# Two expert layers on one core: groups of 256 inner units as the outer loop over all tokens, with the sums in SBUF

## The chip, the cores and the metric

One core of a Trainium2 chip runs the whole program. The metric is the time of one execution on the device in microseconds (us). Engines are named as in the profile: PE is TensorE's products, PEld its loads of the stationary operand, DVE VectorE, ACT ScalarE, POOL GpSimd, SP the engine whose queue issues the DMAs.

## What is computed

Attention over 4 batches, 8 heads, 576 tokens and a head width of 64 (weights below a threshold near the row's greatest are dropped) gives x, 2304 tokens of 512 values. Two expert layers follow, each with 2048 inner units:

```
h = x @ w_in              # 2304 x 512 times 512 x 2048
g = h * sigmoid(1.702 h)  # layer 1;   layer 2: g = max(0.01 h, h)
x = g @ w_out             # 2304 x 2048 times 2048 x 512
```

The weights arrive as float64. The output is float32.

## The kernel before, in words

Products run on TensorE in fp32r, and so that little precision is lost each operand is kept as a high half and a low half: x = xh + xl, w = wh + wl, g = gh + gl. A product is the sum of three: high by high, high by low, low by high. This is why each pass over a 128 x 128 piece of weights costs three matmuls.

The attention (to about 398 us) is ordered by hand in the table START. It is untouched by the change, but for how x is declared (one tile with four parts in place of four tiles). It also converts the weights of the first three blocks of 128 inner units (f = 0, 1, 2) of layer 1, as NA = 3 says.

In the expert layers the order of each engine's instructions is laid out when the program is built, by a planner that goes by the program's order and by when it expects operands and buffers to be ready; on the chip each engine then keeps to that order.

**Weights.** `load_weights` (line 327 on) fetches a block f: `stage` (L286) issues two DMAs of 512 KB on SP's queue into one of three staging buffers (w64), and `convert` turns each of the two pieces from float64 words into float32: ACT takes the magnitude (L300), then DVE runs four operations (L302, L304, L308, L312) on a float buffer wF (two of them), then ACT rounds to the high half (L322) and POOL subtracts to get the low half (L325). The halves (wih, wil, woh, wol) of f = 3 to 15 have 13 slots in the pool wb, so all of a layer's weights are resident.

**Layer 1** runs over five blocks of tokens (WIDTHS: 496, 436, 440, 436, 496), and inside each over the 16 blocks f. For each pair (block, f):
- `split_x` (L816), once for each block: four copies on ACT (L830, xh) and four subtractions on DVE (L828, xl).
- `hidden` (L833): 12 matmuls (L840) into a PSUM buffer h (four of them), ACT's sigmoid (L847), DVE's product gf of h and it (L848), ACT's rounding gh (L852), POOL's subtraction gl (L854).
- `product` (L857): 12 matmuls (L872) into four PSUM accumulators y which stay open over all 16 f.

After the last f, `finish` (L876) copies the four y into x (L881), half on ACT, half on DVE.

**Layer 2** is the same over six blocks of 384 tokens (TILES), with 9 output matmuls of 512 columns for each f (L874; here g is the stationary operand and rows of the output come out), DVE's gf at L851 after ACT's L850, and `finish` copies (L885) and stores (L887, L890).

The loop at L892 to L911 issues hidden one f ahead of product. It loads the weights of f = 5 to 15 of layer 1 during layer 1's first block of tokens, two f ahead (L901), and the weights of all 16 f of layer 2 during layer 1's last block, each f after its last use (L909).

Of the kernel before, what the change touches and what calls it, by code (L numbers as in the profile page):

```python
# [23 lines left out]
NA = 3  # blocks of 128 hidden units whose first weights have room during the attention  # L24
SB = 3  # staging buffers
TB = 496  # tokens of a block at the most
# Blocks of tokens: the first layer's by their widths, the second's as three tiles of rows of the
# output, (batch, i) for rows 4p + i and (batch, 4) for the last 64 rows of two batches.
WIDTHS = (496, 436, 440, 436, 496)
TILES = [[(b, i) for i in range(3)] for b in range(3)]  # L30
TILES += [[(0, 3), (1, 3), (2, 3)], [(3, 3), (0, 4), (2, 4)], [(3, 0), (3, 1), (3, 2)]]
HI_MAX = 15 * 2.0**13 - 2.0**-7  # of a float64's high word as float32, where the value is float32's greatest
# How a tile of probabilities gets its low part: "D" VectorE; "P" GpSimd, from a copy; "PP" GpSimd
# makes both parts from the copy.
LO = ("P", "P", "PP", "P", "D", "P", "D", "P", "P")
# the engine of each threshold, the buffers of v, of the probabilities and of the scores, and the
# products that bring TensorE to speed
# [4 lines left out]
# The order of the attention phase's steps, by position: a pair of heads starts PERIOD after the one  # L42
# before it, and pairs with an order of their own have it under their number.
# [196 lines left out]
def attention_moe_moe(  # L240
# [23 lines left out]
    x = [cp.tile([P, NTOK], F32, name=f"x{c}") for c in range(NCB)]  # L264

    # tau as a threshold offset that is never negative, and the scale of the scores:
    # with tau < 0 nothing reaches the threshold and every key weighs the same.
# [9 lines left out]
    def stage(layer, f, n):  # L277
        """A block of weights of 128 hidden units on its way into SBUF."""
        m = 2 if wide else 1
        w = weights[layer][n].bitcast(I32) if wide else weights[layer][n]  # L280
        if n == 0:
            src = w[:, f * P * m : (f + 1) * P * m].rearrange("(c p) x -> p c x", p=P)
        else:
            src = w[f * P : (f + 1) * P, :].rearrange("p (c x) -> p c x", c=NCB)
        t = stg.tile([P, DM * m], I32 if wide else F32, tag="w64", name=f"w{layer}_{f}_{n}", bufs=SB)
        nc.sync.dma_start(split(t, NCB), src)  # L286
        staged[layer, f, n] = t

    def convert(layer, f, n, part):
        src = staged[layer, f, n]  # L290
        if wide:
            # float64 to float32 by bits, magnitudes brought into float32's range
# [42 lines left out]
    # A pair of heads shares its tiles of 128 tokens: 0-3 the first head's, 4 the last 64 tokens  # L335
    # of both, 5-8 the second head's. Column i * 128 + p of x is token 4p + i of a batch, and
    # column 512 + r is token 512 + r.
    with tc.tile_pool(name="at", bufs=1) as at, tc.manual_schedule():
# [74 lines left out]
        # tiles of scores: head and block of 128 rows; the middle one has the last 64 rows of both  # L413
# [101 lines left out]
        def halves(p, t):  # L515
            """Source bank and the two destinations of a tile's transposed probabilities."""
# [36 lines left out]
        def corner(pt, src):  # L553
            """Both 64 by 64 halves of src transposed, each in its own partitions."""
# [151 lines left out]
        # The first pair's operands are made by whichever engine is free: the second head's tiles  # L706
        # (part A) before the rest (part B), and both orders of the halves of k instead of a swap.
# [69 lines left out]
        # the activation table and TensorE's clock are up before the first operands come  # L777
# [17 lines left out]
    ml = ctx.enter_context(tc.tile_pool(name="ml", bufs=2, reuse_waits="tile"))  # L795
    wb = ctx.enter_context(tc.tile_pool(name="wb", bufs=NF - NA, reuse_waits="tile"))

    xs_of, g_of, y_of = {}, {}, {}

    def pieces(layer, blk):  # L800
        """Columns of a block and, for each run of them, where they are in x."""
        if layer == 1:
            c0 = sum(WIDTHS[:blk])
            w = WIDTHS[blk]
            return w, [(slice(0, w), 1, lambda t: t[:, c0 : c0 + w])]
        (b, i), second = TILES[blk][:2]
        if second == (b, i + 1):
            return 384, [(slice(0, 384), 1, lambda t: t[:, b * S : b * S + 384])]
        if i == second[1]:
            return 384, [(slice(0, 384), 3, lambda t: split(t, B)[:, b : b + 3, i * P : i * P + P])]  # L810
        return 384, [
            (slice(0, P), 1, lambda t: t[:, b * S + i * P : b * S + i * P + P]),
            (slice(P, 384), 4, lambda t: split(t, B)[:, :, 512:S]),
        ]

    def split_x(layer, blk):  # L816
        w, runs = pieces(layer, blk)
        hs, ls = (
            [ml.tile([P, TB], F32R, tag=f"x{n}{c}", name=f"x{n}{layer}_{blk}_{c}", bufs=1)[:, 0:w] for c in range(NCB)]
            for n in "hl"  # L820
        )
        for low in range(2):
            for c in range(NCB):
                for cols, n, at_x in runs:
                    src = at_x(x[c])
                    hi, lo = (t[c][:, cols] if n == 1 else split(t[c][:, cols], n) for t in (hs, ls))
                    if low:
                        nc.vector.tensor_tensor(out=lo, in0=src, in1=hi, op=ALU.subtract)  # L828
                    else:
                        nc.scalar.copy(hi, src)  # L830
        xs_of[layer, blk] = (w, hs, ls)

    def hidden(layer, blk, f):  # L833
# [10 lines left out]
        gh = ml.tile([P, TB], F32R, tag="gh", name=f"gh{n}")[:, 0:w]  # L844
        gl = ml.tile([P, TB], F32R, tag="gl", name=f"gl{n}")[:, 0:w]
# [7 lines left out]
        last = (layer, blk, f) == units[-1]  # L853
# [3 lines left out]
    def product(layer, blk, f):  # L857
        w = xs_of[layer, blk][0]
        gh, gl = g_of.pop((layer, blk, f))
        woh, wol = wslot[layer, f][2:4]  # L860
        if f == 0:
            two = [ps.tile([P, 2, 512], F32, tag="s", name=f"y{layer}_{blk}_{e}", bufs=2) for e in range(2)]
            y_of[layer, blk] = [two[e // 2][:, e % 2, :] for e in range(NCB if layer == 1 else w // P)]
        ys = y_of[layer, blk]
        terms = [(i, e) for i in range(3) for e in range(len(ys))]
        if (layer, blk, f) == units[-1]:
            terms.sort(key=lambda z: z[1])
        for i, e in terms:
            wt, g = ((woh, gh), (wol, gh), (woh, gl))[i]
            first, last = f == 0 and i == 0, f == NF - 1 and i == 2  # L870
            if layer == 1:
                nc.tensor.matmul(ys[e][:, 0:w], lhsT=wt[:, e * P : (e + 1) * P], rhs=g, start=first, stop=last)  # L872
            else:
                nc.tensor.matmul(ys[e], lhsT=g[:, e * P : (e + 1) * P], rhs=wt, start=first, stop=last)  # L874

    def finish(layer, blk):  # L876
        ys = y_of.pop((layer, blk))
        if layer == 1:
            w, ((_, _, at_x),) = pieces(layer, blk)
            for e, y in enumerate(ys):  # L880
                (nc.vector.tensor_copy if e % 2 else nc.scalar.copy)(at_x(x[e]), y[:, 0:w])  # L881
            return
        for e, (y, (b, i)) in enumerate(zip(ys, TILES[blk])):
            o = stg.tile([P, 2 * DM], F32, tag="w64", name=f"o{blk}_{e}", bufs=SB)[:, 0:DM]
            (nc.vector.tensor_copy if e % 2 else nc.scalar.copy)(o, y)  # L885
            if i < 4:
                nc.sync.dma_start(out[b * S : b * S + 512, :].rearrange("(p i) e -> p i e", i=4)[:, i, :], o)  # L887
            else:
                for j in range(2):
                    nc.sync.dma_start(out[(b + j) * S + 512 : (b + j + 1) * S, :], o[64 * j : 64 * j + 64, :])  # L890

    units = [(l, blk, f) for l, n in ((1, len(WIDTHS)), (2, len(TILES))) for blk in range(n) for f in range(NF)]  # L892
    split_x(1, 0)
    for f in range(NA, NF):
        if f < NA + 2:
            load_weights(1, f)
    hidden(*units[0])
    for n, u in enumerate(units):
        l, blk, f = u
        if l == 1 and blk == 0 and f + 2 >= NA + 2 and f + 2 < NF:  # L900
            load_weights(1, f + 2)  # L901
        if n + 1 < len(units):
            nl, nb, nf = units[n + 1]
            if nf == 0:
                split_x(nl, nb)
            hidden(nl, nb, nf)
# [33 lines left out]
```

## Time and profile before

| what | us |
|---|---|
| median of three runs (1257.3 to 1259.44) | 1257.49 |
| span of the profiled execution, first to last instruction | 1252.7 |
| what lies between the two | 4.8 |
| first matmul of the expert layers | 397.68 |
| TensorE busy in the span | 1190.8 |

The page gives no time of the profiled execution beside its span. To read the profile: a busy share is the time that an engine has at least one instruction in work. Matmuls overlap one another (a new one enters while the one before drains), so the length of one matmul is longer than the distance to the next, and the distance is what counts. The granted clock of TensorE is given as a share of its full speed of 2.4 GHz.

### The profile page before, as it was taken

The numbers are of one execution on the slowest core, as the hardware profiler recorded it, in microseconds if no ns is written. First come the engines' busy times: TensorE is split into PE (matmuls) and PEld (weight loads), VectorE is DVE, ScalarE is ACT, GpSimd is POOL, SyncE is SP. The second block draws the span as 40 slices with busy tenths as digits, with TensorE's granted clock in tenths as the row PEclk, the third lists the DMA queues.
The fourth block names the chain that finished last, engine by engine and source line by source line (L and its number), as shares of the span: only waits on it lengthen the run. The fifth ranks groups of instructions, "written<-read, shape, count | busy, mean of one in ns | idle before, by whom it ended". The sixth has DMA issues, their size and how long they took to land.

```text
span 1252.7 us, 17393 instructions
## 1 busy us (share of the span) xinstructions
PE 1190.8 (95%) x6361; PEld 1033.3 (82%) x6361; DVE 703.1 (56%) x1322; ACT 603.3 (48%) x1133; POOL 640.8 (51%) x583
## 2 busy tenths in 40 slices
PE   6989999999998888999999999888999999999998
PEld 5778888888776665999999988667999999999987
DVE  7899999999999988512112138898121212121211
ACT  6778888888885544323222244445222323232322
POOL 5899999999986555322222235555222222222221
PEclk9799999999999999999999999999999999999999
DMA  4422213232112343200000003432000000000100
GB/s 129 117 63 70 74 50 87 56 76 68 48 30 67 119 125 128 66 1 1 1 1 1 1 18 118 133 110 77 1 26 1 26 1 26 1 26 1 26 1 26
DMA packets 47493, 62.40 MB, mean 50 GB/s; under 512 B 10416, under 2 KB 39088, under 8 KB 47408
## 3 DMA queue, kind: packets, MB, share of 16 engines
q1 hardware_dynamic: 47408, 61.29, 16.8%
q8 instruction: 50, 0.82, 0.3%
q14 instruction: 35, 0.29, 0.1%
HBM read 47.71 MB, written 4.72 MB: 42 GB/s over the span
## 4 chain that ended last, share of the span: by engine, by line
PE 56%; POOL 18%; DVE 17%; issue 5%; ACT 2%; DMA 1%; SPq 0%; POOLq 0%; ACTq 0%; DVEq 0%
PE h L840 25%; PE y L874 15%; PE y L872 10%; POOL ptg0l L550 5%; DVE wF L308 4%; POOL ptg1l L550 4%; DVE wF L312 3%; DVE wF L304 3%; DVE wF L302 2%; POOL thr L477 2%; PE pv L585 2%; POOL rb L634 1%; DVE pp L491 1%; POOL khl L376 1%; POOL vhl L376 1%
## 5 line engine op out<-in xcount | busy, mean ns | idle before, releaser
L854 POOL TENSOR_TENSOR gl<-gf,gh 128x384 fp32r<-128x384 f32 (+3 forms) x175 | 199.4, 1140 | 475.9 <-ACT gh L852 403.8
L851 DVE TENSOR_TENSOR gf<-h,gf 128x384 f32<-128x384 f32 x96 | 53.4, 556 | 287.5 <-ACT gf L850 287.5
L840 PE MATMUL h<-xh,wih 128*128 128x384 f32 (+3 forms) x704 | 168.0, 355 | 13.6 <-ACT wih L322 7.6
L840 PE MATMUL h<-xh,wil 128*128 128x384 f32 (+3 forms) x704 | 176.3, 355 | 1.2 <-POOL wil L325 1.2
L840 PE MATMUL h<-xl,wih 128*128 128x384 f32 (+3 forms) x704 | 169.3, 354 | 0.1
L852 ACT CAST gh<-gf 128x384 fp32r<-128x384 f32 (+3 forms) x176 | 95.1, 541 | 118.5 <-DVE gf L851 46.2
L491 DVE SCALAR_TENSOR_TENSOR pp<-sc,thr,e 128x576 f32<-128x576 f32 x128 | 150.7, 1186 | 1.7 <-POOL thr L477 1.1
L840 PEld LDWEIGHTS h<-xh,wih 128*128 128x128 f32 x704 | 128.5, 188 | 26.5 <-ACT wih L322 10.9
L848 DVE TENSOR_TENSOR gf<-h,gf 128x496 f32<-128x496 f32 (+2 forms) x80 | 50.5, 633 | 172.9 <-ACT gf L847 172.8
L850 ACT ACTIVATE gf<-h 128x384 f32<-128x384 f32 x96 | 47.3, 492 | 199.7 <-PE h L840 199.1
L840 PEld LDWEIGHTS h<-xl,wih 128*128 128x128 f32 x704 | 130.1, 189 | 12.7 <-DVE xl L828 0.5
L840 PEld LDWEIGHTS h<-xh,wil 128*128 128x128 f32 x704 | 129.2, 189 | 12.6 <-POOL wil L325 3.7
L470 ACT ACTIVATE e<-s,m 128x576 f32<-128x576 f32 x144 | 107.2, 745 | 33.6 <-DVE sc L457 18.9
L457 DVE TENSOR_SCALAR_CACHE_REDUCE sc<-s 128x576 f32<-128x576 f32 x144 | 107.1, 750 | 6.9 <-PE s L429 3.8
L429 PE MATMUL s<-kt,qt 128*128 128x288 f32 x512 | 99.1, 320 | 10.4 <-ACT e L470 8.0
L847 ACT ACTIVATE gf<-h 128x496 f32<-128x496 f32 (+2 forms) x80 | 44.1, 553 | 119.5 <-PE h L840 117.7
L872 PE MATMUL y<-gh,woh 128*128 128x496 f32 (+2 forms) x320 | 83.0, 379 | 12.5 <-ACT gh L852 12.4
L550 POOL TENSOR_TENSOR ptg0l<-raw,ptg0h 128x512 fp32r<-128x512 f32 x64 | 92.1, 1441 | 0.3 <-ACT ptg0h L543 0.3
L429 PEld LDWEIGHTS s<-kt,qt 128*128 128x128 f32 x512 | 73.3, 191 | 17.2 <-ACT e L470 14.4
L874 PE MATMUL y<-woh,gh 128*128 128x512 f32 x288 | 82.8, 394 | 3.9 <-DVE x L881 2.6
L512 PE MATMUL pp<-ident,pp 128*128 128x128 f32 x512 | 79.1, 283 | 5.9 <-DVE pp L491 4.4
L874 PE MATMUL y<-woh,gl 128*128 128x512 f32 x288 | 83.2, 396 | 0.9 <-POOL gl L854 0.9
(122 smaller groups left out, 2250.4 us busy)
## 6 DMA issues: line engine op xcount, KB each, us to landing
w<-in_moe_w_in_dram SPq DMA_DIRECT2D x32, 512.0 KB, 3.7
w<-in_moe_w_out_dram SPq DMA_DIRECT2D x32, 512.0 KB, 3.5
kt<-kt SPq DMA_DIRECT2D x30, 288.0 KB, 4.1
kn<-in_k_dram SPq DMA_DIRECT2D x16, 256.0 KB, 2.9
qn<-in_q_dram SPq DMA_DIRECT2D x16, 256.0 KB, 2.8
vn<-in_v_dram SPq DMA_DIRECT2D x16, 256.0 KB, 3.0
out_dram<-o SPq DMA_DIRECT2D x16, 256.0 KB, 2.3
kn<-in_k_dram SPq DMA_DIRECT2D x32, 16.0 KB, 2.6
```

Source lines behind the costliest of these rows:

```text
L429: nc.tensor.matmul(sc[:, a, 0:HALF], lhsT=w, rhs=kt[n][:, c : c + HALF], start=n == 0, stop=n == 1)
L457: nc.vector.tensor_scalar(out=split(r["sc", t], 2), in0=r["s", t][:, :, 0:HALF], scalar1=1.0, scalar2=3.0e38, op0=ALU.mult, op1=ALU.min, a ...
L470: nc.scalar.activation(split(e, 2), r.pop(("s", t))[:, :, 0:HALF], AF.Exp, bias=r["m"][:, t : t + 1], scale=-1.0)
L491: nc.vector.scalar_tensor_tensor(out=dst, in0=r.pop(("sc", t)), scalar=r["thr"][:, t : t + 1], in1=r.pop(("e", t)), op0=ALU.is_le, op1=ALU ...
L512: nc.tensor.transpose(pt[:, j * P : (j + 1) * P], src[:, off + j * P : off + (j + 1) * P], ident)
L550: nc.gpsimd.tensor_tensor(out=lo, in0=split(st[p].pop(("raw", t)), 4), in1=hi, op=ALU.subtract)
L840: nc.tensor.matmul(h, lhsT=wt[:, c * P : (c + 1) * P], rhs=xx[c], start=i == 0 and c == 0, stop=i == 2 and c == NCB - 1)
L851: nc.vector.tensor_tensor(out=gf, in0=h, in1=gf, op=ALU.max)
L852: nc.scalar.copy(gh, gf)
L854: (nc.vector if last else nc.gpsimd).tensor_tensor(out=gl, in0=gf, in1=gh, op=ALU.subtract)
L872: nc.tensor.matmul(ys[e][:, 0:w], lhsT=wt[:, e * P : (e + 1) * P], rhs=g, start=first, stop=last)
L874: nc.tensor.matmul(ys[e], lhsT=g[:, e * P : (e + 1) * P], rhs=wt, start=first, stop=last)
```

## The change

In the expert layers the loops change places. The outer loop is now over groups of G = 2 blocks f, 256 inner units, eight groups for each layer; the inner loop is over all tokens, in five blocks of at most 512 (four of 512, one of 256), in both layers. What is resident changes with it: the xh and xl of all tokens are kept (a buffer for each block of tokens), and wb has four slots in place of 13. PSUM now sums over one group only (six matmuls for each output tile), and the tile is then added to a sum in SBUF, which lies in x itself: group 0 copies (half on ACT, half on DVE), later groups add on DVE. In the last group of layer 2 the DVE add writes the output tile o, which is stored in pieces of consecutive rows. y has two buffers, one for each output tile in work, gh and gl four each. Weights are loaded two groups ahead of their use, in the first two steps of each group. Comments are removed too. The core of the diff:

```diff
-NA = 3  # blocks of 128 hidden units whose first weights have room during the attention
-TB = 496  # tokens of a block at the most
-WIDTHS = (496, 436, 440, 436, 496)
+TB = 512
+G = 2
...
-    x = [cp.tile([P, NTOK], F32, name=f"x{c}") for c in range(NCB)]
+    xx_all = cp.tile([P, NCB, NTOK], F32, name="x")
+    x = [xx_all[:, c, :] for c in range(NCB)]
...
-    wb = ctx.enter_context(tc.tile_pool(name="wb", bufs=NF - NA, reuse_waits="tile"))
+    wb = ctx.enter_context(tc.tile_pool(name="wb", bufs=2 * G, reuse_waits="tile"))
...
+    def product(layer, grp, blk, e):
         w = xs_of[layer, blk][0]
+        cols = span(blk)
+        y = ps.tile([P, 2, 512], F32, tag="s", name=f"y{layer}_{grp}_{blk}_{e}", bufs=2)[:, 0, :]
+        n = 0
+        for i in range(3):
+            for f in range(grp * G, grp * G + G):
+                gh, gl = g_of[layer, blk, f]
+                woh, wol = wslot[layer, f][2:4]
+                wt, g = ((woh, gh), (wol, gh), (woh, gl))[i]
...
+                if layer == 1:
+                    nc.tensor.matmul(y[:, 0:w], lhsT=wt[:, at_e], rhs=g, start=first, stop=last)
+                else:
+                    nc.tensor.matmul(y, lhsT=g[:, at_e], rhs=wt, start=first, stop=last)
...
+        if grp == 0:
+            (nc.vector.tensor_copy if e % 2 else nc.scalar.copy)(acc, y)
+        elif layer == 1 or grp < NF // G - 1:
+            nc.vector.tensor_tensor(out=acc, in0=y, in1=acc, op=ALU.add)
+        else:
             o = stg.tile([P, 2 * DM], F32, tag="w64", name=f"o{blk}_{e}", bufs=SB)[:, 0:DM]
+            nc.vector.tensor_tensor(out=o if w == TB else split(o, 2), in0=y, in1=acc, op=ALU.add)
+            store(o, cols.start + e * P)
...
+    steps = [(l, g, blk) for l in (1, 2) for g in range(NF // G) for blk in range(NB)]
...
+    weights_until(2 * G)
+    lead(steps[0])
+    lead(steps[1])
+    for j in range(G):
+        hidden(*steps[0], j)
+    for n, (l, g, blk) in enumerate(steps):
+        nxt = steps[n + 1] if n + 1 < len(steps) else None
+        if n + 2 < len(steps):
+            lead(steps[n + 2])
+        ne = outputs(l, blk)
+        per = (ne + G - 1) // G
+        for j in range(G):
+            if nxt:
+                hidden(*nxt, j)
+            for e in range(j * per, min(ne, (j + 1) * per)):
+                product(l, g, blk, e)
+        if blk < G:
+            weights_until((((l - 1) * NF) // G + g + 1) * G + G + blk + 1)
```

`lead` calls `split_x` for a block of tokens in group 0 of a layer, `weights_until(n)` calls `load_weights` up to the n-th block of both layers, and `outputs` gives the output tiles of a block of tokens: four, or two for the narrow block of layer 2.

## Rows read from the trace of the kernel before

**Rows 1.** The profile page: the span, the busy time of each engine with its share of the span, and TensorE's busy tenths in 40 slices of 31.3 us.
```profile
span 1252.7 us, 17393 instructions
...
PE 1190.8 (95%) x6361; PEld 1033.3 (82%) x6361; DVE 703.1 (56%) x1322; ACT 603.3 (48%) x1133; POOL 640.8 (51%) x583
...
PE   6989999999998888999999999888999999999998
```
**Rows 2.** Busy times by stretch of the expert layers. Columns: the stretch, its length, then for PE, PEld, DVE, ACT and POOL the busy us and the number of instructions, TensorE's granted clock, the DMA engines' busy share, GB/s.
```profile
397.70:510.00 112.30, 95.50 (x392) 72.54 (x393) 102.19 (x130) 53.72 (x91) 58.31 (x41) 0.98 0.39 122
510.00:738.00 228.00, 228.00 (x1145) 214.72 (x1144) 42.83 (x72) 61.84 (x115) 55.47 (x49) 1.00 0.02 5
738.00:850.00 112.00, 101.71 (x439) 83.02 (x437) 94.86 (x122) 54.68 (x95) 60.26 (x43) 0.97 0.37 113
850.00:920.00 70.00, 66.02 (x325) 58.41 (x326) 30.47 (x47) 25.15 (x51) 25.46 (x22) 1.00 0.10 31
920.00:1247.50 327.50, 327.50 (x1640) 296.15 (x1638) 54.32 (x103) 88.56 (x185) 79.37 (x78) 1.00 0.03 11
```
**Rows 3.** What TensorE waited for, from 396 to 560 us (first four) and from 700 to 900 us (the last); from 900 us to the end this view has no row. Columns: us in total, times, the longest.
```profile
PE h L840 <- ACT wih L322: 7.6, 7, 2.0
PE y L872 <- ACT gh L852: 5.2, 6, 1.4
PE h L840 <- DVE gf L848: 2.1, 1, 2.1
PE h L840 <- ACT xh L830: 1.6, 1, 1.6
...
PE y L874 <- DVE x L881: 2.6, 1, 2.6
```
**Rows 4.** ACT's timeline: the copies of finished sums that end a block of tokens, five of layer 1 and the first two of layer 2. Columns: start, busy us, what.
```profile
515.45 1.04 ACT L881 COPY x<-y 128x496 f32<-128x496 f32 x2
...
589.53 0.95 ACT L881 COPY x<-y 128x436 f32<-128x436 f32 x2 [1.14 <-PE y L872]
...
665.99 0.96 ACT L881 COPY x<-y 128x440 f32<-128x440 f32 x2 [1.15 <-PE y L872]
...
742.91 0.94 ACT L881 COPY x<-y 128x436 f32<-128x436 f32 x2
...
848.68 1.04 ACT L881 COPY x<-y 128x496 f32<-128x496 f32 x2
...
916.90 1.08 ACT L885 COPY o<-y 128x512 f32<-128x512 f32 x2 [0.70 <-PE y L874]
...
983.86 1.07 ACT L885 COPY o<-y 128x512 f32<-128x512 f32 x2 [0.70 <-PE y L874]
```
**Rows 5.** The timeline at the start of the expert layers (their first matmuls, and ACT's table load ahead of the first sigmoid) and at their end (the last two matmuls).
```profile
397.68 1.17 PE L840 MATMUL h<-xh,wih 128*128 128x496 f32 x4 [1.62 <-ACT xh L830]
...
408.14 1.28 ACT L847 ACT_TABLE_LOAD   x1
...
1247.03 0.63 PE L874 MATMUL y<-woh,gl 128*128 128x512 f32 x2
```
**Rows 6.** The source line L585, the attention's products of 256 columns: the durations in ns of a weight load, of a matmul and of a separate semaphore step on TensorE (least, median, greatest).
```profile
L585 PEld LDWEIGHTS pv<-ptg0h,vhl x128: 186/188/333, 32.9 to 387.7; 128*128 128x128 f32 x128
L585 PE MATMUL pv<-ptg0h,vhl x128: 274/283/581, 33.1 to 387.8; 128*128 128x256 f32 x128
...
L585 PEldq EVENT_SEMAPHORE  x34: 51/51/51, 32.1 to 391.2; - x34
```
**Rows 7.** TensorE's timeline in the attention (the first row) and in layer 2 (the others): runs of four matmuls, with the start of the first and the time from there to the end of the fourth.
```profile
204.65 0.64 PE L585 MATMUL pv<-ptg0h,vhl 128*128 128x256 f32 x4
...
1002.73 0.86 PE L840 MATMUL h<-xh,wih 128*128 128x384 f32 x4
1003.43 0.86 PE L840 MATMUL h<-xh,wil 128*128 128x384 f32 x4
```
**Rows 8.** VectorE's groups of instructions from 397.7 us to the end. Columns: busy us and mean ns of one, then the idle time before them.
```profile
L308 DVE SCALAR_TENSOR_TENSOR wF<-w,wF 128x512 int32<-128x512 int32 x58 | 64.5, 1113 | 1.3
...
L312 DVE SCALAR_TENSOR_TENSOR wF<-w,wF 128x512 int32<-128x512 int32 x58 | 51.8, 892 | 1.2
L848 DVE TENSOR_TENSOR gf<-h,gf 128x496 f32<-128x496 f32 (+2 forms) x80 | 50.5, 633 | 172.9 <-ACT gf L847 172.8
L304 DVE TENSOR_SCALAR wF<-wF 128x512 int32<-128x512 int32 x57 | 47.3, 830 | 1.2
L302 DVE TENSOR_SCALAR wF<-wF 128x512 f32<-128x512 f32 x57 | 34.5, 605 | 21.6 <-ACT wF L300 21.6
...
L885 DVE COPY o<-y 128x512 f32<-128x512 f32 x6 | 4.1, 692 | 11.9 <-ACT o L885 11.9
```
**Rows 9.** VectorE's timeline in the first layer's last block: one conversion of a piece of weights (L302, L304, L308, L312) and a product gf (L848).
```profile
787.31 0.42 DVE L302 TENSOR_SCALAR wF<-wF 128x512 f32<-128x512 f32 x1
787.77 0.43 DVE L304 TENSOR_SCALAR wF<-wF 128x512 int32<-128x512 int32 x1
788.23 1.74 DVE L308 SCALAR_TENSOR_TENSOR wF<-w,wF 128x512 int32<-128x512 int32 x1
789.89 0.66 DVE L848 TENSOR_TENSOR gf<-h,gf 128x496 f32<-128x496 f32 x1
790.47 0.68 DVE L312 SCALAR_TENSOR_TENSOR wF<-w,wF 128x512 int32<-128x512 int32 x1
```

More of the change, by code (lines that the diff above doesn't have):

```diff
@@ L25 @@
 SB = 3
-TB = 496
-WIDTHS = (496, 436, 440, 436, 496)
-TILES = [[(b, i) for i in range(3)] for b in range(3)]
-TILES += [[(0, 3), (1, 3), (2, 3)], [(3, 3), (0, 4), (2, 4)], [(3, 0), (3, 1), (3, 2)]]
+TB = 512
+G = 2
 HI_MAX = 15 * 2.0**13 - 2.0**-7
@@ L795, in attention_moe_moe, with span @@
     ml = ctx.enter_context(tc.tile_pool(name="ml", bufs=2, reuse_waits="tile"))
-    wb = ctx.enter_context(tc.tile_pool(name="wb", bufs=NF - NA, reuse_waits="tile"))
[L798 to L814, printed above, removed]
+    wb = ctx.enter_context(tc.tile_pool(name="wb", bufs=2 * G, reuse_waits="tile"))
+    xs_of, g_of = {}, {}
+    NB = (NTOK + TB - 1) // TB
+    def span(blk):
+        return slice(blk * TB, min(NTOK, (blk + 1) * TB))
     def split_x(layer, blk):
-        w, runs = pieces(layer, blk)
+        cols = span(blk)
+        w = cols.stop - cols.start
         hs, ls = (
-            [ml.tile([P, TB], F32R, tag=f"x{n}{c}", name=f"x{n}{layer}_{blk}_{c}", bufs=1)[:, 0:w] for c in range(NCB)]
+            [ml.tile([P, w], F32R, tag=f"x{n}{c}_{blk}", name=f"x{n}{layer}_{blk}_{c}", bufs=1) for c in range(NCB)]
             for n in "hl"
@@ L823, in split_x, with hidden @@
             for c in range(NCB):
[L824 to L830, printed above, removed]
+                if low:
+                    nc.vector.tensor_tensor(out=ls[c], in0=x[c][:, cols], in1=hs[c], op=ALU.subtract)
+                else:
+                    nc.scalar.copy(hs[c], x[c][:, cols])
         xs_of[layer, blk] = (w, hs, ls)
-    def hidden(layer, blk, f):
+    def hidden(layer, grp, blk, j):
+        f = grp * G + j
         w, hs, ls = xs_of[layer, blk]
@@ L843, in hidden @@
         gf = ml.tile([P, TB], F32, tag="gf", name=f"gf{n}")[:, 0:w]
-        gh = ml.tile([P, TB], F32R, tag="gh", name=f"gh{n}")[:, 0:w]
-        gl = ml.tile([P, TB], F32R, tag="gl", name=f"gl{n}")[:, 0:w]
+        gh = ml.tile([P, TB], F32R, tag="gh", name=f"gh{n}", bufs=2 * G)[:, 0:w]
+        gl = ml.tile([P, TB], F32R, tag="gl", name=f"gl{n}", bufs=2 * G)[:, 0:w]
         if layer == 1:
@@ L852, in hidden, with outputs @@
         nc.scalar.copy(gh, gf)
-        last = (layer, blk, f) == units[-1]
+        last = (layer, grp, blk, j) == (2, NF // G - 1, NB - 1, G - 1)
         (nc.vector if last else nc.gpsimd).tensor_tensor(out=gl, in0=gf, in1=gh, op=ALU.subtract)
         g_of[layer, blk, f] = (gh, gl)
-    def product(layer, blk, f):
+    def outputs(layer, blk):
+        return NCB if layer == 1 else xs_of[layer, blk][0] // P
+    def product(layer, grp, blk, e):
         w = xs_of[layer, blk][0]
[L859 to L872, printed above, removed]
-            else:
-                nc.tensor.matmul(ys[e], lhsT=g[:, e * P : (e + 1) * P], rhs=wt, start=first, stop=last)
@@ L876, in finish @@
[L876 to L906, printed above, removed]
-        product(*u)
-        if l == 1 and blk == len(WIDTHS) - 1:
-            load_weights(2, f)
-        if f == NF - 1:
-            finish(l, blk)
+        cols = span(blk)
@@ new lines, in product @@
+        y = ps.tile([P, 2, 512], F32, tag="s", name=f"y{layer}_{grp}_{blk}_{e}", bufs=2)[:, 0, :]
[5 more added lines that the diff above has]
+                wt, g = ((woh, gh), (wol, gh), (woh, gl))[i]
+                at_e = slice(e * P, (e + 1) * P)
+                first, last = n == 0, n == 3 * G - 1
+                if layer == 1:
+                    nc.tensor.matmul(y[:, 0:w], lhsT=wt[:, at_e], rhs=g, start=first, stop=last)
+                else:
+                    nc.tensor.matmul(y, lhsT=g[:, at_e], rhs=wt, start=first, stop=last)
+                n += 1
@@ new lines, in product @@
+        if layer == 1:
+            acc, y = x[e][:, cols], y[:, 0:w]
+        elif w == TB:
+            acc = x[e][:, cols]
+        else:
+            acc = xx_all[:, 2 * e : 2 * e + 2, cols]
+            y = split(y, 2)
+        if grp == 0:
+            (nc.vector.tensor_copy if e % 2 else nc.scalar.copy)(acc, y)
+        elif layer == 1 or grp < NF // G - 1:
+            nc.vector.tensor_tensor(out=acc, in0=y, in1=acc, op=ALU.add)
+        else:
+            o = stg.tile([P, 2 * DM], F32, tag="w64", name=f"o{blk}_{e}", bufs=SB)[:, 0:DM]
+            nc.vector.tensor_tensor(out=o if w == TB else split(o, 2), in0=y, in1=acc, op=ALU.add)
+            store(o, cols.start + e * P)
@@ new lines, in store @@
+    def store(o, c0):
+        done = 0
+        while done < P:
+            b, r = divmod(c0 + done, S)
+            if r < 512:
+                i, p0 = divmod(r, P)
+                n = min(P - done, P - p0)
+                dst = out[b * S : b * S + 512, :].rearrange("(p i) e -> p i e", i=4)[p0 : p0 + n, i, :]
+            else:
+                n = min(P - done, S - r)
+                dst = out[b * S + r : b * S + r + n, :]
+            nc.sync.dma_start(dst, o[done : done + n, :])
+            done += n
@@ new lines, in attention_moe_moe, with weights_until, lead @@
+    steps = [(l, g, blk) for l in (1, 2) for g in range(NF // G) for blk in range(NB)]
+    order = [(l, f) for l in (1, 2) for f in range(NF)]
+    ready = NA
+    def weights_until(n):
+        nonlocal ready
+        while ready < min(n, len(order)):
+            load_weights(*order[ready])
+            ready += 1
+    def lead(step):
+        l, g, blk = step
+        if g == 0:
+            split_x(l, blk)
+    weights_until(2 * G)
[3 more added lines that the diff above has]
+        hidden(*steps[0], j)
```

## The prediction, made before the change was run

> **What bounds the kernel now.** I read the busy shares and the 40 slices first, then a table by stretches, then TensorE's waits, then single lines for prices. Over the whole span TensorE is busy for 95% and no other engine for more than 56%, but its slices fall below nine in two places after the attention's end at about 398 us [rows 1]. The change touches only the expert layers, so their stretch is the one to cost. The table by stretches [rows 2] shows the dents: from 510 to 738 and from 920 to 1247.5 TensorE never idles; from 397.7 to 510 and from 738 to 850 VectorE is busy for 91% and 85%, data moves at 113 GB/s and more, and TensorE issues fewer products. Those two are the first layer's first block, whose weights are converted while it runs, and its last block, in which the second layer's weights are converted. The waits say the same [rows 3]: in these stretches TensorE waits for a rounded weight (wih) and for activations (gh) that stand behind conversions on VectorE; from 900 to the end it has no wait at all.
>
> **How much is lost.** A steady block of 440 tokens lasts 665.99 - 589.53 = 76.46 us [rows 4] for 16 x 24 products, 199.1 ns each. 440 columns at 2.4 GHz, the level granted there (clock 1.00), are 183.3 ns, so a product costs its columns and 15.8 ns. A steady block of the second layer lasts 66.96 us [rows 4] for 16 x (12 products of 384 and 9 of 512 columns): 16.4 ns on top of the columns. With these, the first layer (2304 x 24 x 16 columns = 368.6 us, 1920 products) should take 399.0 us, the second (184.3 + 184.3 us of columns, 1152 + 864 products) 401.7, together 800.7. TensorE began at 397.7 and issued its last product at 1247.3 [rows 5], so it was done, by its pitch, at 1247.5: 849.8 us. So 49.1 us are lost. The interval from 742.91 to 848.68 [rows 4] is 105.8 us where the pitch gives 84.9: 20.9 lost. Block 0, from 397.7 to 515.45, has most of the rest.
>
> **The change part by part.**
> Products. Layer 1 keeps 5 blocks x 16 x 24 = 1920 products and the same columns (four blocks of 512, one of 256): 399.0 us. Layer 2 goes from six blocks of 384 to the same five: hidden products fall from 1152 to 960, output products stay 864 of 512 columns. 368.6 + 1824 x 0.0164 = 398.5. Sum 797.5, 3.2 us less than before. The narrow block is not held up by its narrower products: four of them run in 0.64 us [rows 7], the last 0.28 long [rows 6], so 0.12 each, 13 ns above their columns.
> How far the weight loads hide decides the 192 saved products. Rows show 384-column products 176 ns apart (0.70 us for four) [rows 7], 160 ns of columns and 16 more, though each has a weight load of its own. [...]
>
> Weights. Before, 29 blocks of weights (f = 3 to 15 of layer 1, all 16 of layer 2) were converted inside the two dents. Now each pair is converted while another group runs, and a group lasts 399 / 8 = 50 us. One conversion is four VectorE operations, 0.605 + 0.830 + 1.113 + 0.892 = 3.44 us on average [rows 8], two for each block: 6.9 us, against 5.3 us of TensorE for one f of a 496-token block. That is why it did not hide. In the new order a group needs 4 x 3.44 = 13.8 us in 50. So the whole 49.1 us can go.
>
> Sums. Every group now ends in an evacuation: 160 in layer 1 and 144 in layer 2, 19 of them copies on ScalarE. The operation (PSUM plus SBUF into SBUF) has no row; the bounds are the same engine's product of h and gf, 0.633 us [rows 8], and its copy of 512 columns from PSUM, 0.692 [rows 8]. I take 0.69, as the widths match: about 188 us. VectorE's total in the expert stretch: 101 (gf) + 188 + 58 x 3.44 = 200 + 24 (splits) = 513 us, 64% of 797.5. The widest group takes 6.3 + 13.8 + 13.8 = 34 of 50 us. ScalarE loses 22 copies of results and gains 19; GpSimd's work stays the old, and neither is busy for more than 54% of any of the stretches [rows 2]. These additions lie beside TensorE.
>
> What is late next: y has two buffers only. Buffer one is filled by product e0 (6 x 0.23 = 1.38 us) and needed again by e2, after e1 (1.38) and the next hidden (12 x 0.23 = 2.76): 4.1 us, of which the add needs 0.69. So VectorE may reach it 3.4 us late. One whole conversion (3.44) ahead of an add costs nothing, two cost about 3.5 us of TensorE. In the second dent VectorE ran three conversion operations, 2.6 us, in a row ahead of a gf [rows 9]. Bounds: 0, and the 49 us that the same 29 blocks cost when VectorE was 85 to 91% busy. With 64%, and a group's time to spare, I take 6 us, nearer to nothing.
> Waits. Each product's first matmul now waits for a buffer: 304 more waits. In steady stretches waits for free buffers show no idle time [rows 3]; a separate semaphore step takes 0.051 us [rows 6]. Bounds 0 and 15 us; I take 0, since the steady pitch already has such waits in it.
> Start. Sixteen splits and two hidden parts come before the first product, and the sigmoid's table load of 1.28 us [rows 5]. Before, TensorE waited 1.6 us for the first xh and 2.1 for a gf [rows 3]. Bounds 0 and 5; I take 1.5.
> Layer change. Block 0 of layer 2 is split one step before it is needed; the wait of 2.6 us for x [rows 3] goes, and it is in the 49.1.
> DMA. The weights move in the same pieces on SP's queue; two blocks took some 14 us at 113 to 122 GB/s [rows 2] and have 50. Output tiles go out in two or three pieces each, spread over the last group's 50 us. The end: last product, an add (0.69) instead of a copy (0.69 [rows 8]), two stores instead of three. I leave the 5.2 us from TensorE's end to the span's.
>
> **Sum.** 397.7 + 797.5 + 1.5 + 6 + 5.2 = 1207.9 us of span. The profiled execution has a span of 1252.7 [rows 1], 4.8 below the median of 1257.5; the page gives no other time of its own, so I carry the 4.8: **1213 us**, 3.5% less.
>
> **Rivals.**
> 1. *The adds come late, a little everywhere.* For it: conversions were bunched in front of gf's before [rows 9], and weights of a group become free to be written all at once, at its end. If each of the 29 blocks costs 1 us of TensorE instead of 0.2: 1213 - 6 + 29 = 1236.
> 2. *VectorE's order becomes the bound (slower).* The place is the add behind two or more conversions, with TensorE stopped at the next y. One such stop is 3.5 us; 15 of them give the gain back, which is one in every group, or 0.16 us on each of 304 products. With one for each of the 29 blocks, 101 us: 1308. [...] Against it: 36% of VectorE's time is free, and the order put that gf ahead of that conversion's last operation.
> 3. *Weight loads that don't hide.* If a load's 188 ns [rows 6] stood between products, fewer and wider products would save 192 x 0.188 = 36 us instead of 3: 1180. The spacing there [rows 7] excludes nearly all of it. [...]
> 4. *The dents stay*, because the conversions are held up until their group needs them: about 1257. A lead of a whole group speaks against it.
>
> **How the numbers follow.** Forecast 0.72, rival 1 0.15, rival 2 0.08, rival 3 0.02, rival 4 0.03. The forecast's own ends are 1205 (no start, no lateness) and 1222 (15 us of waits); 2 us below for scatter between runs. The range goes from 1203 to 1238 and takes in rival 1. A measurement of this kernel tells about 0.2% from no change. Faster 0.89, same 0.03, slower 0.08.
>
> **What would show it.** Right: TensorE in nines from 398 us to the end, a span of the expert stretch near 805 us, VectorE at six tenths throughout instead of one and nine, data moving at some 25 GB/s almost to the end, adds near 0.69 us, and few waits of TensorE for VectorE. Wrong: TensorE waits for the evacuating add of several us per group (rival 1 or 2), pitch of 512-column products other than 0.23 us, adds far above 0.7 us, or waits for wih in a group's first step.

## The result, and the profile after

The changed kernel takes **1226.57 us** (median of 4 runs, 1225.85 to 1227.46) where the one before takes 1257.78 beside it (1257.3 to 1259.44): a ratio of 0.9748, 95% interval 0.9735 to 0.9762, 2.5% faster. The point forecast was 1213, 13.6 us too low. The profiled execution took 1227.46 with a span of 1225.2.

The page after, in the manner of [rows 1], with VectorE's slices (30.6 us each):
```profile
span 1225.2 us, 17168 instructions
...
PE 1174.8 (96%) x6169; PEld 974.5 (80%) x6169; DVE 841.8 (69%) x1567; ACT 589.4 (48%) x1090; POOL 637.2 (52%) x567
...
PE   6899999999999989999999999899999999999998
...
DVE  7999999999997882463755649786244574654344
```
The two broad dents of before have shrunk to slices of eight at the start of the expert layers and at the change of layer, and VectorE is still at eight and nine in the same two places. The stretches that answer to [rows 2]:
```profile
397.70:510.00 112.30, 105.49 (x480) 86.06 (x479) 71.81 (x109) 49.63 (x91) 41.79 (x28) 0.96 0.17 52
510.00:738.00 228.00, 224.34 (x1087) 188.50 (x1086) 126.24 (x198) 69.74 (x126) 77.01 (x63) 1.00 0.11 35
738.00:850.00 112.00, 105.31 (x495) 86.11 (x494) 89.46 (x140) 49.94 (x91) 46.07 (x34) 0.98 0.21 66
850.00:920.00 70.00, 70.00 (x328) 58.63 (x327) 24.95 (x40) 19.92 (x37) 17.96 (x15) 1.00 0.07 23
920.00:1220.50 300.50, 297.71 (x1375) 247.36 (x1373) 154.69 (x236) 84.88 (x154) 93.25 (x78) 1.00 0.12 35
```
TensorE gained 10 us of busy time in the first stretch and 3.6 in the third, and idles 3.7 and 2.8 us in the second and the last, where it idled nothing before. VectorE's work is spread, but not evenly: it is 80% busy from 738 to 850 and 36% in the 70 us after. What TensorE waited for from 396 us to the end (L826 is the hidden matmul, L859 and L861 the products, L874 the adds, L872 the first group's copies, L834 and L837 the ops that write gf, L877 the last group's adds, L815 the split of x), in place of [rows 3]:
```profile
PE y L859 <- DVE x L874: 8.7, 9, 2.0
PE h L826 <- DVE gf L834: 5.0, 5, 1.8
PE h L826 <- DVE gf L837: 2.5, 3, 0.8
PE y L859 <- DVE x L872: 1.6, 3, 0.8
PE y L859 <- ACT x L872: 1.4, 1, 1.4
PE h L826 <- ACT xh L815: 0.5, 1, 0.5
PE y L861 <- DVE o L877: 0.3, 1, 0.3
```
No wait for a rounded weight is left (7.6 us before); 18.1 of the 20.0 us are for VectorE. By stretch: 6.4 us up to 450, 4.8 from 450 to 750, 6.1 from 750 to 850, 2.8 from there to the end. VectorE's groups in place of [rows 8]:
```profile
L874 DVE TENSOR_TENSOR x<-y,x 128x512 f32<-128x512 f32 (+1 forms) x248 | 162.8, 657 | 216.3 <-PE y L861 108.9 <-PE y L859 106.4
...
L305 DVE SCALAR_TENSOR_TENSOR wF<-w,wF 128x512 int32<-128x512 int32 x58 | 47.8, 826 | 0.8
...
L301 DVE TENSOR_SCALAR wF<-wF 128x512 int32<-128x512 int32 x58 | 43.8, 757 | 0.9
L299 DVE TENSOR_SCALAR wF<-wF 128x512 f32<-128x512 f32 x58 | 36.5, 629 | 14.9 <-ACT wF L297 14.3
```
Adds waited 216 us for TensorE in all. VectorE had time to spare, and TensorE waited for it all the same. How that comes about is seen best in one of the three equal stalls of layer 2 (at 1004.28, 1054.58 and 1104.87 us, one in each of three groups). TensorE's timeline, then VectorE's, GpSimd's and ScalarE's:
```profile
1002.83 0.61 PE L861 MATMUL y<-woh,gl 128*128 128x512 f32 x2
1004.28 1.20 PE L826 MATMUL h<-xh,wih 128*128 128x512 f32 x4 [0.83 <-DVE gf L837]
```
```profile
995.15 0.41 DVE L301 TENSOR_SCALAR wF<-wF 128x512 int32<-128x512 int32 x1
...
1000.72 0.75 DVE L299 TENSOR_SCALAR wF<-wF 128x512 f32<-128x512 f32 x1 [0.36 <-ACT wF L297]
1001.50 1.40 DVE L301 TENSOR_SCALAR wF<-wF 128x512 int32<-128x512 int32 x1
1002.93 0.69 DVE L305 SCALAR_TENSOR_TENSOR wF<-w,wF 128x512 int32<-128x512 int32 x1
1003.54 0.68 DVE L837 TENSOR_TENSOR gf<-h,gf 128x512 f32<-128x512 f32 x1
1004.14 0.68 DVE L874 TENSOR_TENSOR x<-y,x 128x512 f32<-128x512 f32 x1
```
```profile
999.87 2.74 POOL L840 TENSOR_TENSOR gl<-gf,gh 128x512 fp32r<-128x512 f32 x2
```
```profile
997.92 0.62 ACT L319 CAST wih<-wF 128x512 fp32r<-128x512 f32 x1 [5.08 <-PE h L826]
...
1001.22 0.60 ACT L836 ACTIVATE gf<-h 128x512 f32<-128x512 f32 x1 [0.53 <-POOL gl L840]
```
ScalarE's rounding of one piece (L319) had waited 5.08 us until the last hidden products with the old weights were through and their slot came free; the next piece follows behind it, at the turn from one group to the next. Three conversion ops of that piece (2.8 us) stand ahead of the gf. The gf's input was ready at 1001.82; TensorE needs the h buffer at about 1003.3 and goes on at 1004.28. So this gf, 0.68 us long, had some 0.8 us to spare (an estimate from these rows) and began 1.7 us after its input.

**The start and the clock.** The first expert matmul, in place of [rows 5], begins 3.5 us later than before:
```profile
401.22 1.22 PE L826 MATMUL h<-xh,wih 128*128 128x512 f32 x2 [0.47 <-ACT xh L815]
```
The end of the attention ran at a lower granted clock here (0.50, before 1.00). Two stretches after:
```profile
382.00:386.00 4.00, 1.60 (x13) 0.98 (x10) 3.94 (x8) 3.38 (x7) 2.79 (x3) 0.91 0.00 0
386.00:391.00 5.00, 5.00 (x19) 3.76 (x19) 3.24 (x7) 1.01 (x2) 3.95 (x4) 0.50 0.25 70
```
and the same before:
```profile
382.00:386.00 4.00, 2.91 (x18) 1.97 (x17) 4.00 (x9) 2.88 (x6) 3.77 (x4) 1.00 0.00 0
386.00:391.00 5.00, 3.69 (x23) 2.83 (x23) 4.70 (x10) 2.77 (x7) 3.20 (x5) 1.00 0.09 11
```
TensorE had been less busy just ahead (1.60 of 4 us, before 2.91), then was granted 0.50 until about 405.8 us (0.55 from 404 to 406). The products of 512 columns from 401.8 on stood 0.43 us apart till then, about 0.23 from 406 us on; some 2.3 us lost.

### The profile page after: what moved, and what is told of

Read it like the earlier page. It is cut to its first block, busy times and chain, and to the rows that moved or that the text cites. A ratio compares the mean times of both kernels' runs of the same rounds, so it can differ in the third digit from the quotient of the medians.

```text
span 1225.2 us, 17168 instructions
## 1 busy us (share of the span) xinstructions
PE 1174.8 (96%) x6169; PEld 974.5 (80%) x6169; DVE 841.8 (69%) x1567; ACT 589.4 (48%) x1090; POOL 637.2 (52%) x567
## 4 chain that ended last, share of the span: by engine, by line
PE 60%; POOL 18%; DVE 12%; issue 5%; ACT 3%; DMA 1%; SPq 0%; POOLq 0%; ACTq 0%; DVEq 0%
PE h L826 28%; PE y L861 15%; PE y L859 12%; POOL ptg0l L547 4%; POOL ptg1l L547 4%; DVE wF L305 2%; PE pv L582 2%; POOL thr L474 2%; DVE wF L299 2%; POOL rb L631 1%; DVE wF L309 1%; DVE wF L301 1%; DVE pp L488 1%; POOL khl L373 1%; POOL vhl L373 1%
## 5 line engine op out<-in xcount | busy, mean ns | idle before, releaser
L840 POOL TENSOR_TENSOR gl<-gf,gh 128x512 fp32r<-128x512 f32 (+1 forms) x159 | 194.3, 1242 | 426.2 <-PE y L861 219.9
L874 DVE TENSOR_TENSOR x<-y,x 128x512 f32<-128x512 f32 (+1 forms) x248 | 162.8, 657 | 216.3 <-PE y L861 108.9
L838 ACT CAST gh<-gf 128x512 fp32r<-128x512 f32 (+1 forms) x160 | 85.6, 576 | 304.8 <-PE y L861 162.9
L826 PE MATMUL h<-xh,wih 128*128 128x512 f32 (+1 forms) x640 | 161.8, 373 | 8.0 <-DVE gf L834 5.0
L826 PE MATMUL h<-xh,wil 128*128 128x512 f32 (+1 forms) x640 | 168.9, 371 | 0.0
L826 PE MATMUL h<-xl,wih 128*128 128x512 f32 (+1 forms) x640 | 163.0, 369 | 0.0
L826 PEld LDWEIGHTS h<-xh,wih 128*128 128x128 f32 x640 | 114.2, 190 | 31.9 <-DVE gf L834 7.1
L826 PEld LDWEIGHTS h<-xh,wil 128*128 128x128 f32 x640 | 116.8, 190 | 22.1
L826 PEld LDWEIGHTS h<-xl,wih 128*128 128x128 f32 x640 | 115.7, 189 | 21.3
L859 PE MATMUL y<-gh,woh 128*128 128x512 f32 (+1 forms) x320 | 93.7, 374 | 11.7 <-DVE x L874 8.7
L859 PE MATMUL y<-gh,wol 128*128 128x512 f32 (+1 forms) x320 | 92.0, 369 | 0.0
L859 PE MATMUL y<-gl,woh 128*128 128x512 f32 (+1 forms) x320 | 92.0, 368 | 0.0
L861 PE MATMUL y<-woh,gh 128*128 128x512 f32 x288 | 89.2, 391 | 0.3 <-DVE o L877 0.3
L861 PE MATMUL y<-wol,gh 128*128 128x512 f32 x288 | 88.9, 390 | 0.0
L861 PE MATMUL y<-woh,gl 128*128 128x512 f32 x288 | 88.8, 389 | 0.0
```

What stands on the lines that cost most here:

```text
L826: nc.tensor.matmul(h, lhsT=wt[:, c * P : (c + 1) * P], rhs=xx[c], start=i == 0 and c == 0, stop=i == 2 and c == NCB - 1)
L838: nc.scalar.copy(gh, gf)
L840: (nc.vector if last else nc.gpsimd).tensor_tensor(out=gl, in0=gf, in1=gh, op=ALU.subtract)
L859: nc.tensor.matmul(y[:, 0:w], lhsT=wt[:, at_e], rhs=g, start=first, stop=last)
L861: nc.tensor.matmul(y, lhsT=g[:, at_e], rhs=wt, start=first, stop=last)
L874: nc.vector.tensor_tensor(out=acc, in0=y, in1=acc, op=ALU.add)
```

## The experiments

**Theory:** the loss that is left is conversions standing together on VectorE ahead of an add or a gf, which TensorE feels because y has two buffers and a late gf holds an h buffer. **Rival A:** adds out of two buffers come late by themselves, whatever the conversions do. **Rival B:** the loss is the late start and the clock. Each of the first four was timed beside the kernel before at 1258.6 us (1253.59 to 1259.06), each of the last four at 1254.87 (1254.08 to 1260.17); ratios are to those. Differences to the change are of the medians; by the ratios they come out up to 2 us higher or lower.

| kernel | median us (range) | ratio, 95% interval |
|---|---|---|
| the change | 1226.57 (1225.85 to 1227.46) | 0.9748, 0.9735 to 0.9762 |
| before_noconv | 1212.82 (1209.4 to 1214.2) | 0.9648, 0.9619 to 0.9677 |
| after_noconv | 1203.33 (1198.95 to 1205.1) | 0.9572, 0.9541 to 0.9602 |
| after_y4 | 1205.92 (1201.41 to 1207.52) | 0.9592, 0.9561 to 0.9623 |
| after_pieces | 1199.79 (1197.6 to 1202.87) | 0.955, 0.9515 to 0.9584 |
| pieces_bunched | 1222.74 (1221.39 to 1223.03) | 0.9737, 0.9711 to 0.9763 |
| after_all | 1199.08 (1196.16 to 1200.43) | 0.9545, 0.9519 to 0.957 |
| after_splits | 1231.99 (1227.28 to 1234.48) | 0.9805, 0.9774 to 0.9837 |
| after_g1 | 1298.57 (1294.72 to 1299.43) | 1.0334, 1.0306 to 1.0362 |

**1. Conversions left out of both kernels.** `before_noconv` and `after_noconv` skip VectorE's four conversion ops for f from 3 on; loads, rounding on ScalarE and the subtraction on GpSimd stay. The edit, in `load_weights` of each:
```
-            for part in "ABCDKHM":
+            for part in "AHM":
```


> The kernel before, with VectorE's four operations (L302, L304, L308, L312) left out of the conversion of the weights f = 3 and on in both layers: the rounding on ScalarE and the subtraction on GpSimd stay, the weights are wrong. Theory (the 49 us lost in the two dents are VectorE's conversions): the dents go and the time falls by 38 to 46 us, to 1212 to 1220. Rival (the dents come from fetching the weights, or from ScalarE's and GpSimd's part): 1235 or more.

Measured: 45.8 us less than before, as expected, where the prediction put 49.1 down to the conversions. TensorE's waits from 396 us on shrink to one row:
```profile
PE h L840 <- ACT xh L830: 1.6, 1, 1.6
```


> The changed kernel with the same four operations left out. Theory (what the changed kernel still loses against its matmul pitch, 24 us in the trace, is mostly conversions bunched on VectorE ahead of its adds and products): 1226.6 falls by 8 to 14 us, to 1212 to 1219, and comes within 6 us of the kernel before without conversions. Rival A (the adds out of two PSUM buffers cost this by themselves): no more than 3 us less, 1223 or more.

Measured: 23 us less than the change, more than expected: the conversions cost the changed kernel more than its visible waits of TensorE. The first matmul came at 399.64 here, so the start (rival B) gives 1.6 of it. With neither kernel converting, the new order is still 9.5 us better than the old, where at most 6 was expected.

**2. Four buffers for y.** `after_y4` closes the PSUM pool after the attention and opens one in which y is one bank, four times, out of the same room. The new pool also has `reuse_waits="tile"`, which the old one has not.
```
-        y = ps.tile([P, 2, 512], F32, tag="s", ..., bufs=2)[:, 0, :]
+        y = ps.tile([P, 512], F32, tag="y", ..., bufs=4)
```


> The changed kernel with four one-bank buffers for y in place of two; nothing else. Theory (VectorE reaches the adds late because conversions stand ahead of them): more buffers ride over it, TensorE's 12 us of waits for the evacuation of y shrink to under 3 us, 1214 to 1220. Rival B (half-level clock and the start cost the rest): 1224 or more.

Measured: 1205.9, 21 us less with every conversion in place, better than expected. Most of what is left, 7.1 of 8.1 us, lies before 450 us; three of the five rows from 396 us on:
```profile
PE y L862 <- ACT gh L841: 2.2, 2, 1.2
PE y L862 <- DVE x L875: 1.8, 2, 1.2
PE h L829 <- DVE gf L837: 1.6, 1, 1.6
```
The first matmul came at 398.23 here, so 3 of the 21 us are the start's. The order of the instructions changed with the buffers too: gf's now stand ahead of up to four adds, so the run shows what buffers, order and the pool's setting do together.

**3. One piece of weights in each step.** `after_pieces` keeps two buffers and converts one piece (f, n) in each of the four full steps of the group before its use, behind the step's last gf on VectorE's queue; its load is issued a step earlier.
```
-        if blk < G:
-            weights_until(...)
+        if n + 1 in piece: stage(*piece[n + 1])
+        if n in piece:
+            with tc.issue_after(at_dve[0].ins):
+                for part in "ABCDKHM": convert(*piece[n], part)
```


> The changed kernel with the weights converted one piece (f, n) a step, in the four full steps of the group just before their use, each piece queued on VectorE behind the step's last gf; y keeps its two buffers, splits as they were. Theory (bunching): 1213 to 1220, and TensorE's waits in the layer change (750 to 850 us) go from 9 us to under 4. Rival A (two buffers of y are too few whatever the order): 1223 or more.

Measured: 1199.8, far better than expected, and as good as leaving the conversions out (the intervals overlap). Its waits from 396 us on:
```profile
PE y L860 <- DVE x L875: 1.5, 2, 1.2
PE h L827 <- ACT xh L816: 0.5, 1, 0.5
...
```
So two buffers do for the evacuations, which are the same 304: rival A falls. Its first matmul is at 399.45 with the clock as low as in the change, 1.8 us ahead of the change's, so rival B has little of the 27 us either.

**4. The same pieces together.** `pieces_bunched` differs in the place: all four pieces of a group are loaded and converted in the second step of the group before, without the step between load and conversion.
```
-            piece[(k // G - 1) * NB + G * m + k % G] = (*order[k], m)
+            piece.setdefault((k // G - 1) * NB + 1, []).append((order[k], m))
```


> The same work as the kernel with one conversion piece per step (1199.8 us), but all four pieces of a group are converted in one step, the second step of the group before. Theory (conversions queued together on VectorE ahead of adds, with two result buffers): slower than one piece per step by 10 to 30 us, 1210 to 1228, about where the change itself stands (1226.6), with TensorE waiting for the add in the steps that convert. Rival (what helped was only that the order behind the step's last gf was fixed, not the spreading): 1198 to 1204. Rival (the amount of VectorE work sets it): the amount is the same, so also 1198 to 1204.

Measured: 1222.7, 23 us slower than spread, for the same work with the same order hint (`issue_after`). The three largest of its waits from 385 us on; the others are 1.3 us or less, and none is for a weight:
```profile
PE y L860 <- DVE x L875: 8.0, 13, 1.4
PE h L827 <- DVE gf L838: 6.2, 6, 1.0
PE y L862 <- DVE x L873: 1.6, 1, 1.6
...
```
The shorter lead of the loads is not what costs: ScalarE, which takes up each piece first, waited 0.9 us in all for loads from 405 us on. A piece's four operations take 2.77 us on average here and 2.44 where they are spread, so they were also longer; but in experiment 5, with four buffers, they take 2.98 and nothing is lost; what the length alone costs with two buffers was not tried. These two kernels carry the verdict: not the amount of VectorE's work but its bunching.

**5. Everything at once.** `after_all` has the pieces, the four buffers and the splits of experiment 6.


> One conversion piece per step, four one-bank result buffers, and the splits of a later block queued behind the step's own activations, together. Theory: the first already leaves only about 2 us of waits for adds, and both cures act on one loss, so the three don't add up: 1195 to 1201, at most 4 us below the pieces alone (1199.8). Rival (each cures a loss of its own: 27 us by the pieces, 21 by the buffers): the floor of the pitch, 1190 or less.

Measured: 1199.1, no different from the pieces alone. Buffers and spreading cure one and the same loss; they don't add.

**6. Only the splits moved.** `after_splits` queues the splits of the block after next behind the step's own gh and gf; conversions stay as in the change.
```
-        if n + 2 < len(steps): lead(steps[n + 2])
...
+            if j == 0 and n + 2 < len(steps):
+                with tc.issue_after(at_act[0].ins), tc.issue_after(at_dve[0].ins):
+                    lead(steps[n + 2])
```


> Only the splits of x for a later block are queued behind the step's own work on ScalarE and VectorE; conversions stay as the change has them. Theory (conversions are the loss, the splits cost the 3 us of waits for gf in the first block): 1222 to 1227. Rival (the late start of the first block, 9 us by its excess, is all due to the splits): 1215 to 1219.

Measured: 1232.0, 5 us above the change, outside both expectations. The splits now come late themselves. Waits from 396 to 450 us:
```profile
PE h L827 <- ACT xh L816: 4.4, 3, 2.9
PE y L860 <- ACT gh L839: 3.3, 1, 3.3
...
```
With two smaller rows they are 8.4 us, where the change has 6.4: moving splits alone does not cure the start. The pieces kernel did, with the splits where the change has them.

**7. Groups of one f.** `after_g1` sets `G = 1`: 608 evacuations instead of 304, each product half as long. The slots for weights and the buffers of gh and gl, which hang on `G`, halve with it, so the run does not take these apart.


> Groups of one f (128 inner units) instead of two: 608 evacuations instead of 304, so VectorE has about 190 us more to do, some 700 of 797 us, and each product has half as long before the next. Theory (two result buffers and late adds): the interval until a buffer is needed again shrinks by more than a half, so each conversion ahead of an add stops TensorE: 1240 to 1330, slower than the change by 1 to 8 per cent. Rival (adds cost TensorE nothing by themselves, and conversions as much as before): 1222 to 1232.

Measured: 1298.6, 3.3% slower than the kernel before. The waits from 385 us on, largest first:
```profile
PE y L859 <- DVE x L874: 13.6, 36, 1.2
PE h L826 <- DVE gf L834: 6.3, 10, 2.4
PE y L861 <- DVE x L874: 5.9, 30, 0.3
...
```
These and the smaller rows of the experts come to 32.5 us, only 12.5 more than in the change, of the 72 that it lost to it. The rest is in lengthened spacing, as TensorE's timeline shows beside VectorE's:
```profile
1025.59 0.39 PE L861 MATMUL y<-woh,gl 128*128 128x512 f32 x1
1026.16 0.47 PE L861 MATMUL y<-woh,gh 128*128 128x512 f32 x1 [0.18 <-DVE x L874]
...
1027.40 0.40 PE L861 MATMUL y<-woh,gl 128*128 128x512 f32 x1
1027.88 0.51 PE L861 MATMUL y<-woh,gh 128*128 128x512 f32 x1
```
```profile
1025.33 1.38 DVE L874 TENSOR_TENSOR x<-y,x 128x512 f32<-128x512 f32 x2 [1.44 <-PE y L861]
```
The step from 1025.59 to 1026.16 is 0.57 us where 0.23 is usual, and only 0.18 is told as idle; the step to 1027.88 is 0.48 with no idle told at all. A product now takes 0.69 us and its add 0.69, so the buffer is back just when it is wanted, with no time for anything in between.

## Why the prediction was right or wrong

The sign and the range held; the likeliest case did not. **By its mechanism and its size it is rival 1 that happened**, with gf's late as well as adds, and a second error of the other sign hid part of it. With the products as I priced them the time would have been some 1238, the end of the range: that it lay well inside was luck. The terms, against 1212.7 before rounding:

- *Start of the stretch*, 397.7: 401.2, +3.5 us. Not foreseen; the attention's end at the lower clock goes with it.
- *Products*, 797.5: 785.8, so 11.7 too much. I priced each at its columns and 15.8 to 16.4 ns, from blocks of 440 columns and from the second layer's mean of 384 and 512. The pieces kernel, almost free of waits, shows 22 products of 512 columns in 4.98 us, 226.4 ns each:
```profile
1187.92 0.62 PE L862 MATMUL y<-woh,gh 128*128 128x512 f32 x2
...
1192.90 0.61 PE L862 MATMUL y<-woh,gl 128*128 128x512 f32 x2
```
  that is 13.1 on top of the columns, and 256 columns go at 0.119 (twelve in 1.43 us). 3168 x 0.2264 + 576 x 0.119 = 785.8. The two widths lie 256 columns and 107.4 ns apart, 2.4 columns a ns at a granted clock of 1.00.
- *Start, lateness and waits*, 1.5 + 6 + 0: this is the step that failed. TensorE's last product ended at 1220.35, 819.1 us after its first, so 33.3 lie over the products, 25.8 more than forecast: 19.5 us of visible waits (0.5 of the 20.0 lies before the first product), 2.3 of the lower clock, and 11.5 of lengthened spacing that is told as no wait, as in experiment 7. From 406 us on, the steps from one product's start to the next that are over 30 ns longer than these prices lose 27.6 us, of which 19.5 is told as idle; that is 8.1 of the 11.5, and the rest is spread thinly over all other steps. With the conversions spread the same stretch, the low clock in it too, takes 793.9 (399.45 to 1193.35), 25.2 us less. That is 0.87 us for each of the 29 blocks; I took 0.2, rival 1 had 1.
- *Tail*, 5.2: 4.85. *Around the span*, 4.8: 2.3, which I had taken from the difference between a profiled span and the median of other runs.

3.5 - 11.7 + 25.8 - 0.4 - 2.5 = 14.7, against 14.8 between the profiled execution and the sum.

**What held.** The 49.1 us lost before were nearly all the conversions': 45.8 went without them. The evacuations: 162.8 + 12.5 + 12.5 (copies L872 and last adds L877) = 188 us, as forecast. VectorE's total was less than forecast, some 495 us of durations against 513 (467 where overlaps count once), and conversions took 3.03 us each instead of 3.44. No weight was waited for. One figure on DMA was off by its own rows, and nothing hung on it: two blocks are four pieces of 512 KB, which at 113 to 122 GB/s take 17 to 19 us, not 14.

**Where the reasoning broke.** I went from the average (64% busy, 34 of 50 us in the widest group) to a lateness "nearer to nothing", though the slack of 3.4 us that I worked out myself is what two conversions in a row exceed, and though [rows 9] showed how they are ordered. And 3.4 us is the slack of an add: a gf ahead of which conversions stand had 0.8 in the stall shown, less than one piece takes, and 7.5 of the 20.0 us of waits are for gf's. Whether conversions bunch is set by when weights come free and how the order is laid, at the turn from group to group, not by how full the group is. That each conversion was 0.41 us shorter than I took it did not prevent it. The price of bunching for the same work was there to be measured: 23 us.

**Rival 2** was right about its mechanism (in the stall shown VectorE began L305 at 1002.93, ahead of a gf whose input was there at 1001.82) and wrong about this kernel: at groups of two f the stops were short; at groups of one they cost the whole gain and 44 us more. **Rival 3** is excluded again: with 192 loads fewer the order without conversions gained 9.5 us, not 36. **Rival 4** fell with the result.

**Open:** how much of the 3.5 us at the start is due to the clock, and why the attention's end fed TensorE less here. The clock fell at that place (0.50 to 0.59 from 386 to 391 us) in all eight kernels of the experiments, the one before without its conversions among them, so the change's loops alone don't explain it; no run took it apart. Nor was it tried whether bunched pieces with four buffers come down to 1200.

## What to carry to other kernels

When work is moved beside the bottleneck, cost it by the longest run of it that can stand ahead of an operation the bottleneck waits for, against the slack of that operation's buffers, and not by the engine's busy share: 68% and 67% busy gave 1200 and 1223 us here. Either spread it, one piece in each step behind the step's own work, or deepen the buffers; the second cure on top of the first brings nothing. Before splitting a reduction finer, compare the evacuation with the product that hides it: at 1.36 against 0.66 us there was room, at 0.69 none.

## What the runs showed of the hardware that was not expected

The same VectorE operation on weights takes two lengths. In the pieces kernel and in the one with everything (from 405 to 1200 us), the shift of a piece (L301 there, L302 here) is the same instruction on the same tile:
```profile
L301 DVE TENSOR_SCALAR wF<-wF 128x512 int32<-128x512 int32 x58 | 30.0, 516 | 0.6
```
```profile
L302 DVE TENSOR_SCALAR wF<-wF 128x512 int32<-128x512 int32 x58 | 67.9, 1171 | 0.5
```
It averages 516 ns in one and 1171 in the other; the stall above has one of 1.40 us that began while a GpSimd operation was running. The adds out of PSUM show nothing of it: 659 ns on average in the pieces kernel, 656 in the other. The change's trace, from 396 us on, has 58 shifts (L301). 20 of them took 1.32 to 1.52 us: each began while a GpSimd operation was running and ended 0.28 to 0.29 us after it. The other 38 took 0.41 to 0.43 us; no GpSimd operation was running when 36 of them began, and the one running at the start of the other two ended within 0.07 us. The adds L874 of 512 columns took 686 ns on average where they began while a GpSimd operation was running (47 from 405 us on), and 686 where none overlapped them (130). That GpSimd is the cause was not tried by a run. With four buffers the longer shifts cost the whole nothing: the kernel that has them is within 1 us of the pieces kernel. In the change they can count: had the shift of 1.40 us in the stall above taken 0.41, as at 995.15, the gf would have ended at about 1003.2, just before TensorE needed its buffer (an estimate from those rows).
